# Static places and overflow tiles in a routed mixture of experts: 288 places with eight overflow tiles in place of 416 with two

## The chip, the cores and the metric

The kernel runs on one core of a Trainium2 chip. The metric is device time in microseconds for one execution, the median of several; lower is better. TensorE (PE in the profile) multiplies matrices; VectorE (DVE), ScalarE (ACT) and GpSimd (POOL) do element-wise work; SyncE (SP) issues the weight loads, GpSimd the gathers and scatters of rows.

## The reference

Attention over clusters produces 3072 token rows of 512 numbers; then a mixture of eight experts takes each row to the one expert with the largest gate logit. Only the second part, cut to what matters:

```python
N, D, E, F = (3072, 512, 8, 1024)
logits = x @ w_gate
expert_idx = np.argmax(logits, axis=1)
probs = softmax(logits);  gate_w = probs[np.arange(N), expert_idx]
perm = np.argsort(expert_idx, kind='stable');  x_sorted = x[perm]
for e in range(E):
    lo, hi = (boundaries[e], boundaries[e + 1])     # rows of expert e
    h = np.maximum(x_sorted[lo:hi] @ w1[e], 0.0)    # w1[e]: 512 x 1024
    y_sorted[lo:hi] = h @ w2[e]                     # w2[e]: 1024 x 512
out = gate_w[:, None] * y_sorted[inv_perm]
```

How many rows an expert gets depends on the data. For the inputs of this case the counts are 400, 354, 531, 257, 408, 444, 274 and 404.

## The kernel before

The kernel has to be laid out before the counts are known. Each expert has a fixed number of places, full tiles of 128 and one of 32 (`RQ`). Rows that find no place go to overflow tiles of 128, each of one expert, whose number is read from a register at run time. `XU` such tiles are unrolled; a loop behind them takes any others. A place without a token is computed all the same, and its result is not stored.

```python
XU = 2
RQ = 32
FT = (2, 1)          # tiles of experts 0 and 1 that are done early, from the first three batches
NJ = N // E // P     # 3 full tiles
CAP = NJ * P + RQ    # 416 places
NC = E * (NJ + 1) + NX
```

Token numbers of all places come from one-hot matrices: VectorE and GpSimd make them, TensorE multiplies them (`tokens`), VectorE turns the product into indices. `NC` columns for tiles; the GpSimd product is 6 * NC elements a time.

The first layer of a group is either plain (`layer1`) or, by seven half-size products instead of eight, `layer1_s`. The second layer is `pair_s` (seven products over two full tiles), `layer2` for a full tile alone, and `quarters` for the 32 places, in four column groups:

```python
def layer1(g, fbs):
    cols = sum(g["n"])
    per = min(512 // cols, (fbs[1] - fbs[0]) // 2)
    for f0 in range(fbs[0], fbs[1], 2 * per):
        hp = wide()                                  # PSUM tile of two banks, three buffers
        ...                                          # 4 matmuls a block of 128 features
        for a in range(2):
            if a == 0 and not g.get("scalar_only"):
                nc.vector.tensor_relu(dst, src)
            else:
                nc.scalar.activation(dst, src, AF.Relu)

def quarters(g):
    ...                                              # matmuls into zq, four strips of 32 rows
    for t in range(1, P // RQ):
        nc.scalar.copy(zc[:, t, :], zq[t * RQ : (t + 1) * RQ, :])
    nc.vector.tensor_tensor(zc[:, 0, :], zc[:, 1, :], zq[0:RQ, :], op=ALU.add)
    for t in range(2, P // RQ):
        nc.vector.tensor_tensor(zc[:, 0, :], zc[:, 0, :], zc[:, t, :], op=ALU.add)
    rows_out(g, last, RQ, zc[:, 0, :])               # ScalarE scales by the gate, GpSimd scatters

def seven(mul, a, s, b, t, u, u3, view, c, ready, steps):
    nc.scalar.copy(u, product(s[1], t[1]));  more()  # more(): one step of other VectorE work
    p = product(a[0], b[0]);  add(u, u, p)
    nc.scalar.copy(c11, p);  more()
    add(u3, u, product(s[2], t[2]));  more()
    ...                                              # four products more
```

The sums that the seven products need are made on VectorE: `sums_w1` and `sums_x` (4 operations each) for the first layer, `sums_h` and `sums_w2` for the second.

Weights of one layer are a block of 2 MB; two buffers each for w1 and w2, all loads from SyncE's queue in the order of the code.

Experts 0 and 1 are started early, in the shadow of the attention of the last batch: two tiles and one tile. The main loop runs over groups: the rest of 0, the rest of 1, experts 2 to 7, and two overflow tiles.

```python
for i, g in enumerate(groups):
    if i + 1 < ng:
        n = groups[i + 1]
        steps = sums_h(g) + sums_w2(g) if by_s(i) else []
        ...                       # first layer of i + 1, with these steps between its products
    if i + 3 < ng:
        groups[i + 3]["w"] = [fetch1(groups[i + 3]["e"], i + 3)]
    n = groups[i + 2] if i + 2 < ng else None
    steps = sums_w1(n) if by_s(i + 2) else []
    ...                           # pair_s(g, steps)
    if n is not None:
        turn_of(n)                # transposes of i + 2
        if i + 4 < ng:
            gather_of(groups[i + 4])
        if by_s(i + 2):
            steps += sums_x(n)
    for f in steps:
        f()
    layer2(g, rest)               # third tile and the 32 places
    if n is not None:
        n["w"].append(fetch2(n["e"], i + 2))
```

Of the kernel before, what the change touches and what calls it, by code (L numbers as in the profile page):

```python
# [18 lines left out]

BIG = float(2**60)  # L20
NB = 6
XU = 2
RQ = 32
FT = (2, 1)
NP = sum(FT)


def in_general(tc, ident, ident_b, first_c, first_e, wpool, q, k, v, centroids, w_gate, w1, w2, out):
# [156 lines left out]
def kernel(  # L185
# [11 lines left out]
    nc = tc.nc  # L197
# [16 lines left out]
    XW = Dm + 4  # L214
    assert D == 64 and C == 16 and H * C == P and NQ % 2 == 0 and NQ * P == S and DB * P == Dm and FB * P == F

    NJ = N // E // P
    CAP = NJ * P + RQ
    NX = -(-(N - CAP) // P) + 1
    NC = E * (NJ + 1) + NX  # L220
# [41 lines left out]
    ps_o = late.enter_context(tc.tile_pool(name="ps_o", bufs=1, space=PSUM))  # L262
    ps_m = late.enter_context(tc.tile_pool(name="ps_m", bufs=1, space=PSUM))

    pools = dict(s=ps_s, rows=p1)


    def wide():
# [67 lines left out]
    def quarters(g):  # L336

        last = len(g["n"]) - 1
        zq = wide()[:, 0, :]
        n = FB * RQ // P  # L340
        for i in range(n):
            for t in range(P // RQ):
                nc.tensor.matmul(
                    zq[t * RQ : (t + 1) * RQ, :], lhsT=g["h"][:, t * n + i, last * P : last * P + RQ],
                    rhs=g["w"][1][:, t * n + i, :], start=(i == 0), stop=(i == n - 1),
                )

        zc = pools["wk"].tile([RQ, P // RQ, Dm], F32, name="zc", bufs=1)
        for t in range(1, P // RQ):
            nc.scalar.copy(zc[:, t, :], zq[t * RQ : (t + 1) * RQ, :])  # L350
        nc.vector.tensor_tensor(zc[:, 0, :], zc[:, 1, :], zq[0:RQ, :], op=ALU.add)  # L351
        for t in range(2, P // RQ):
            nc.vector.tensor_tensor(zc[:, 0, :], zc[:, 0, :], zc[:, t, :], op=ALU.add)
        rows_out(g, last, RQ, zc[:, 0, :])

    def layer2(g, tiles=None):
        for j in range(len(g["n"])) if tiles is None else tiles:
            if g["n"][j] < P:
                quarters(g)
                continue  # L360
            zp = wide()[:, 0, :]
            for fb in range(FB):
                nc.tensor.matmul(  # L363
                    zp, lhsT=g["h"][:, fb, j * P : (j + 1) * P], rhs=g["w"][1][:, fb, :],
                    start=(fb == 0), stop=(fb == FB - 1),
                )
            rows_out(g, j, P, zp)
# [48 lines left out]
        return sums_b(g["xs"], *b_of1(g))  # L416

    def sums_h(g):
        t = p1.tile([P, FB, 2 * P], F32, name="hs", bufs=1).rearrange("p a (b t) -> p a b t", t=P)
        g["hs"] = [t[:, 2 * i : 2 * i + 2].rearrange("p a b t -> p (a b) t") for i in range(4)]  # L420
        return sums_a(g["hs"], *a_of2(g))

    def sums_w2(g):
# [43 lines left out]
    def layer1_s(g, steps):  # L467
        half = sum(g["n"]) // 2
        per = FH // 2

        def mul(ps, a, b):
            for f in range(FH):
                o = ps[:, f // per, f % per * half : (f % per + 1) * half]
                for c in range(KH):
                    nc.tensor.matmul(  # L475
                        o, lhsT=a[:, c, f * P : (f + 1) * P], rhs=b[:, c, :],
                        start=(c == 0), stop=(c == KH - 1),
                    )

        four = lambda t: t.rearrange("p (a f) t -> p a f t", a=2)  # L480
        part = lambda f, t: four(g["h"][:, f * FH : (f + 1) * FH, t * half : (t + 1) * half])
        u = p1.tile([P, DB, 2 * P], F32, name="xu", bufs=1).rearrange("p c t -> p (c t)")
        u3 = pools["wk"].tile([P, FB, P], F32, name="u3").rearrange("p c t -> p (c t)")
        u, u3 = (four(t[:, 0 : FH * half].rearrange("p (f t) -> p f t", t=half)) for t in (u, u3))

        c = [part(f, t) for f in range(2) for t in range(2)]
        seven(
            mul, a_of1(g), g["w1s"], b_of1(g), g["xs"], u, u3,
            lambda ps: ps[:, :, 0 : per * half].rearrange("p a (f t) -> p a f t", t=half), c,
            lambda i: nc.scalar.activation(c[i], c[i], AF.Relu), steps,  # L490
        )

    def pair_s(g, steps):
# [4 lines left out]
                    ps[:, 0, 0:DH], lhsT=a[:, f, :], rhs=b[:, f, :], start=(f == 0), stop=(f == FH - 1),  # L498
                )

        uu = p1.tile([P, 2, XW], F32, name="xg1", bufs=1)
        zo = [pools["rows"].tile([P, Dm], F32, name="zo", bufs=4) for j in range(2)]

        def ready(i):
# [13 lines left out]
    def cols_of(t, c0):  # L518
        return lambda j: t[:, c0 + j : c0 + j + 1]
# [9 lines left out]
    def place_consts():  # L529
# [6 lines left out]
        for part in parts:  # L536
            nc.gpsimd.memset(part["keep"], 1.0)
            nc.gpsimd.memset(part["keep"][:, :, 0:1], 0.0)

        nc.gpsimd.memset(firsts, 0.0)  # L540
        for e, n in enumerate(FT):
            nc.gpsimd.memset(firsts[:, e : e + 1], float(n * P))
        k_["b1off"] = iota("b1off", [P, E], [[(NJ + 1) * P, E]], -1, 0)
        k_["b2off"] = iota("b2off", [P, E], [[-(NJ + 1) * P, E]], E * (NJ + 1) * P - CAP, 0)
        k_["thr"] = iota("thr", [P, NX], [[P, NX]], CAP, 0)
        k_["kx"] = iota("kx", [1, NX], [[1, NX]], 0, 0)
        k_["iota"] = iota("iota_f", [P, P], [[1, P]], 0, 0)
        k_["tiles"] = consts.tile([P, NP], F32, name="tiles1")
        for e, n in enumerate(FT):
            for j in range(n):  # L550
                i = sum(FT[:e]) + j
                nc.gpsimd.memset(k_["tiles"][:, i : i + 1], float(e * (NJ + 1) + j))

        tok_i = consts.tile([P, B, NQ], I32, name="tok_i")
        nc.gpsimd.iota(tok_i, pattern=[[S, B], [1, NQ]], base=1, channel_multiplier=NQ)
# [90 lines left out]
    def indices(pool, ps, w, gi, si):  # L646
# [10 lines left out]
        nc.vector.tensor_copy(si, tv)  # L657

    groups1 = [
        dict(  # L660
            n=[P] * n, rows=NF * P, e=e, gi=cols_of(g_idx1, sum(FT[:e])), si=cols_of(s_idx1, sum(FT[:e])), apart=True,
            scalar_only=True,
        ) for e, n in enumerate(FT)
    ]

    msched = ExitStack()
# [1 line left out]
    with ExitStack() as actx:  # L668
# [369 lines left out]

        def gather1(i):
            g = groups1[i]  # L1040
            g["xg"] = p1.tile([P, 2, XW], F32, name="xg1", bufs=1) if i == 0 else p1.tile([P, 1, XW], F32, name="xg2", bufs=1)
            gather(g)

        def turn_rows1(i):
            g = groups1[i]
            g["xT"] = p1.tile([P, DB, 2 * P], F32, name="xu", bufs=1) if i == 0 else p1.tile([P, DB, P], F32, name="xT2", bufs=1)
            g["gate"] = p1.tile([P, FT[i]], F32, name=f"gate{i}", bufs=1)
            turn_rows(g)

        def first_half(i, f0=0, f1=FB):  # L1050
            g = groups1[i]
            if f0 == 0:
                g["w"] = weights[i]
                g["h"] = p1.tile([P, FB, 2 * P], F32, name="hs", bufs=1)
            layer1(g, (f0, f1))

        n = (NG - HP) * TG
# [43 lines left out]

    mctx = ExitStack()
    pools["sums"] = mctx.enter_context(tc.tile_pool(name="sums", bufs=1))
    with tc.tile_pool(name="sm", bufs=1) as sm:
        front, back = parts
        choose(sm, back)
# [28 lines left out]
        for t0 in range(0, NT, TQ):  # L1135
            one_hots(sm, rc, slice(t0, t0 + TQ), k_["iota"], oh_r, oh_c)
        layer2(groups1[0])
        tok_ps = ps_m.tile([P, 512], F32, name="mps")[:, 0 : 2 * NC]
        tokens(tok_ps, oh_r, oh_c, NT)
        indices(sm, tok_ps, NC, g_idx, s_idx)  # L1140
# [47 lines left out]
        g["h"] = pools["wk"].tile([P, FB, CAP], F32, name="h_sb", bufs=2)  # L1188
        layer1(g, (0, FB))

    groups = []
    for e in range(E):
        j0 = FT[e] if e < len(FT) else 0
        c0 = e * (NJ + 1) + j0
        groups.append(dict(n=[P] * (NJ - j0) + [RQ], rows=N, e=e, gi=cols_of(g_idx, c0), si=cols_of(s_idx, c0), apart=True))
    for x in range(XU):
        ex = nc.sync.value_load(xe[0:1, x : x + 1], min_val=0, max_val=E - 1)
        xc = E * (NJ + 1) + x
        groups.append(dict(n=[P], rows=N, e=ex, gi=cols_of(g_idx, xc), si=cols_of(s_idx, xc), apart=True))
    for i in range(2):  # L1200
        gather_of(groups[i])
    for i in range(2):
        groups[i]["w"] = weights[i]
    ng = len(groups)
    by_s = lambda i: 0 < i < E
    for f in sums_w1(groups[1]):
        f()
    layer2(groups1[1])
    g = groups[0]
    g["xT"] = p1.tile([P, DB, 2 * P], F32, name="xu", bufs=1)  # L1210
    turn_of(g)
    gather_of(groups[2])
    g["h"] = pools["wk"].tile([P, FB, CAP], F32, name="h_sb", bufs=2)
# [3 lines left out]
    for f in sums_x(groups[1]):  # L1217
        f()
    layer1(g, (FB // 2, FB))
    groups[2]["w"] = [fetch1(groups[2]["e"], 2)]  # L1220
    for i, g in enumerate(groups):

        if i + 1 < ng:
            n = groups[i + 1]
            steps = sums_h(g) + sums_w2(g) if by_s(i) else []
            if by_s(i + 1):
                n["h"] = pools["wk"].tile([P, FB, CAP], F32, name="h_sb", bufs=2)
                layer1_s(n, steps)
            else:
                n["scalar_only"] = True  # L1230
                for f in steps:
                    f()
                layer1_of(n)
        if i + 3 < ng:
            groups[i + 3]["w"] = [fetch1(groups[i + 3]["e"], i + 3)]
        n = groups[i + 2] if i + 2 < ng else None
        steps = sums_w1(n) if by_s(i + 2) else []
        if by_s(i):
            pair_s(g, steps)
            rest = range(2, len(g["n"]))  # L1240
        else:
            rest = range(len(g["n"]))
        if n is not None:
            turn_of(n)
            if i + 4 < ng:
                gather_of(groups[i + 4])
            if by_s(i + 2):
                steps += sums_x(n)
        for f in steps:
            f()  # L1250
        layer2(g, rest)
        if n is not None:
            n["w"].append(fetch2(n["e"], i + 2))
    msched.close()

    mctx.close()
# [54 lines left out]
```

## Time and profile before

| | |
|---|---|
| time, median of 3 (lowest to highest) | 798.7 us (798.4 to 799.66) |
| span of the profiled execution | 802.5 us |
| mean granted TensorE clock | 0.990 |
| bytes read from and written to memory | 68.26 MB, 13.68 MB |
| last output products of attention end (chain, 399.54 + 4.02) | 403.56 |
| last matmuls of the kernel end (timeline, 778.11 + 13.90) | 792.0 |

In the profile a line gives the source line, the engine, the operation and its tiles as output<-inputs; "x16" counts instructions. The chain of work that ended last is followed back from the last instruction: at each step to what released it, or to the instruction before it on its engine. Where it stays on one engine with no gap, that engine's work is what sets the time there. An idle bracket in a timeline names the wait before a group and the instruction that ended it.

### The profile page before, as it was taken

What the parts mean: (1) busy time and instruction counts of PE and PEld (TensorE: products, weight loads), DVE (VectorE), ACT (ScalarE), POOL (GpSimd) and SP (SyncE); (2) the same over time, 40 slices, a digit from 0 to 9 for tenths busy, and PEclk for the clock granted to TensorE, in tenths of its full rate; (3) what the DMA queues carried; (4) which work ended last, traced back from release to release, by engine and by line L of the source; (5) the groups of instructions that cost most, each with busy time, mean ns of one, the idle gap of its engine ahead of it and who ended that gap; (6) DMA issues with size and microseconds to landing.
All of it is one profiled execution on the core that took longest, in us unless ns stands there. A gap on an engine that the chain in (4) does not pass through costs nothing.

```text
span 802.5 us, 11975 instructions
## 1 busy us (share of the span) xinstructions
PE 774.7 (97%) x4813; PEld 505.5 (63%) x4813; DVE 484.0 (60%) x783; ACT 307.1 (38%) x479; POOL 110.1 (14%) x164
## 2 busy tenths in 40 slices
PE   6999999999999999999999899999999999999994
PEld 4545454545444544444575697989797969696861
DVE  3667667767667767787536336867484847471610
ACT  4554654554655554645510123232323232232120
POOL 2200000000000000022005423030303020101010
PEclk8999999999999999999999999999999999999998
DMA  9026420382231222201010347252525233241240
GB/s 217 2 60 238 91 60 24 117 269 60 60 98 45 57 60 60 99 2 40 1 70 37 102 150 267 105 171 105 191 105 175 105 111 154 67 178 57 99 148 17
DMA packets 76191, 81.75 MB, mean 102 GB/s; under 512 B 52831, under 2 KB 56927, under 8 KB 75616
## 3 DMA queue, kind: packets, MB, share of 16 engines
q1 hardware_dynamic: 70208, 60.82, 24.8%
q0 software_dynamic: 5248, 20.04, 7.6%
q8 instruction: 40, 0.66, 0.3%
q14 instruction: 23, 0.19, 0.1%
q10 hardware_dynamic: 672, 0.05, 0.1%
HBM read 68.26 MB, written 13.68 MB: 102 GB/s over the span
## 4 chain that ended last, share of the span: by engine, by line
PE 74%; issue 12%; DVE 7%; POOL 3%; ACT 2%; POOLq 0%; ACTq 0%; DVEq 0%
PE sps L858 15%; PE sps L475 14%; PE O L878 13%; PE sps L497 8%; PE sps L363 4%; PE sps L309 4%; PE sps L861 3%; DVE T L870 3%; PE mps L899 3%; PE sps L790 2%; PE sps L290 2%; PE sps L773 2%; POOL out_dram L327 1%; PE sps L944 1%; PE mps L912 1%
## 5 line engine op out<-in xcount | busy, mean ns | idle before, releaser
L863 ACT ACTIVATE A<-sps 128x768 f32<-128x768 f32 x192 | 153.2, 812 | 53.1 <-PE sps L861 51.9
L858 PE MATMUL sps<-qk 64*128 64x384 f32 x768 | 160.4, 496 | 0.1
L870 DVE TENSOR_TENSOR T<-T,A 128x768 f32<-128x768 f32 x128 | 122.7, 958 | 14.3 <-ACT lsT L905 0.5
L878 PE MATMUL O<-A,v_in 128*64 128x384 f32 x768 | 130.9, 490 | 0.0
L858 PEld LDWEIGHTS sps<-qk 64*128 64x128 f32 x768 | 66.9, 189 | 50.1 <-issue 42.5
L878 PEld LDWEIGHTS O<-A,v_in 128*64 128x64 f32 x768 | 52.3, 137 | 62.7 <-issue 62.6
L327 POOL DMA_INDIRECT out_dram<-zo,s_idx x34 | 33.0, 970 | 255.1 <-ACT zo L509 170.6
L363 PE MATMUL sps<-w,h_sb 128*128 128x512 f32 x144 | 63.6, 596 | 0.0
L861 PE MATMUL sps<-ohT 64*128 64x384 bf16 x384 | 63.6, 325 | 0.0
L866 DVE SCALAR_TENSOR_TENSOR T<-A 128x768 f32<-128x768 f32 x32 | 30.6, 958 | 49.3 <-ACT A L863 49.3
L475 PEld LDWEIGHTS sps<-xs,w1s 128*128 128x128 f32 x336 | 56.4, 190 | 5.7 <-issue 5.7
L475 PE MATMUL sps<-xs,w1s 128*128 128x208 f32 (+1 forms) x336 | 59.4, 333 | 0.6 <-DVE xs L385 0.6
L811 POOL TENSOR_TENSOR sim<-sim,first_c 128x384 f32<-128x384 f32 x16 | 16.0, 1000 | 263.8 <-DVE sim L810 263.8
L490 ACT ACTIVATE h_sb<-h_sb 128x832 f32<-128x832 f32 (+1 forms) x28 | 24.3, 867 | 69.8 <-DVE h_sb L431 69.8
L363 PEld LDWEIGHTS sps<-w,h_sb 128*128 128x128 f32 x144 | 26.7, 190 | 30.8 <-issue 30.6
L273 POOL DMA_INDIRECT xg<-x_rows,g_idx x34 | 36.6, 1078 | 38.5 <-ACT xgT L298 17.1
L497 PE MATMUL sps<-w2s,hs 128*128 128x256 f32 x168 | 38.6, 379 | 1.8 <-DVE w2s L385 1.8
L475 PE MATMUL sps<-xgT,w 128*128 128x208 f32 (+1 forms) x224 | 40.0, 331 | 0.0
L886 ACT COPY xT<-O 128x384 f32<-128x384 f32 x32 | 15.5, 484 | 61.6 <-PE O L878 61.6
L475 PEld LDWEIGHTS sps<-xgT,w 128*128 128x128 f32 x224 | 38.0, 190 | 0.0
L351 DVE TENSOR_TENSOR zc<-zc,sps 32x512 f32<-32x512 f32 x8 | 5.4, 675 | 53.6 <-ACT zc L350 53.6
L323 ACT ACTIVATE zo<-sps,gate 128x512 f32<-128x512 f32 x12 | 8.3, 688 | 73.9 <-PE sps L363 49.7
(246 smaller groups left out, 1063.0 us busy)
## 6 DMA issues: line engine op xcount, KB each, us to landing
w<-in_moe_w_dram SPq DMA_DIRECT2D x20, 2048.0 KB, 8.5
x_rows<-x POOLq DMA_DIRECT2D x4, 1548.0 KB
q_in<-in_q_dram SPq DMA_DIRECT2D x32, 192.0 KB, 4.5
k_in<-in_k_dram SPq DMA_DIRECT2D x32, 192.0 KB, 4.8
v_in<-in_v_dram SPq DMA_DIRECT2D x16, 384.0 KB, 3.3
xg<-x_rows,g_idx POOLq DMA_INDIRECT x34
out_dram<-zo,s_idx POOLq DMA_INDIRECT x34
csb<-in_centroids_dram ACTq DMA_DIRECT2D x1, 32.0 KB, 1.9
```

The source lines that it names most:

```text
L273: nc.gpsimd.indirect_dma_start(out=g["xg"][0:m, j, :], out_offset=None, in_=x_d[0 : g["rows"], :], in_offset=bass.IndirectOffsetOnAxis(ap= ...
L309: nc.tensor.matmul(o, lhsT=g["w"][0][:, c, fb * P : (fb + 1) * P], rhs=g["xT"][:, c, :cols], start=(c == 0), stop=(c == DB - 1),)
L327: ins = nc.gpsimd.indirect_dma_start(out=out[:, :], out_offset=bass.IndirectOffsetOnAxis(ap=g["si"](j)[0:m], axis=0), in_=zo[0:m], in_offs ...
L363: nc.tensor.matmul(zp, lhsT=g["h"][:, fb, j * P : (j + 1) * P], rhs=g["w"][1][:, fb, :], start=(fb == 0), stop=(fb == FB - 1),)
L475: nc.tensor.matmul(o, lhsT=a[:, c, f * P : (f + 1) * P], rhs=b[:, c, :], start=(c == 0), stop=(c == KH - 1),)
L497: nc.tensor.matmul(ps[:, 0, 0:DH], lhsT=a[:, f, :], rhs=b[:, f, :], start=(f == 0), stop=(f == FH - 1),)
L858: nc.tensor.matmul(ps[:, a, 0:HS], lhsT=qk[g][r, 1, ks], rhs=qk[g][r, 0, qs], start=True, stop=False)
L861: nc.tensor.matmul(ps[:, a, 0:HS], lhsT=ohT[g][r, 1, ks], rhs=ohT[g][r, 0, qs], start=False, stop=True)
L863: nc.scalar.activation(A[u], ps[:, :, 0:HS], AF.Exp)
L866: nc.vector.scalar_tensor_tensor(T[g, half], in0=A[u - 1], scalar=1e-9 / P, in1=A[u], op0=ALU.add, op1=ALU.add)
L870: nc.vector.tensor_tensor(T[g, half], T[g, half], A[u], op=ALU.add)
L878: nc.tensor.matmul(O[g, half][a * D : (a + 1) * D, 0:HS], lhsT=rows[g, "v"][:, a, j, :], rhs=a_[:, a, :], start=(j == 0), stop=(j == NQ - 1),)
```

## The change

The fixed places of an expert go from 416 (three tiles and 32) to 288 (two tiles and 32), and the unrolled overflow tiles from two to eight. What a place costs is paid whether a token fills it or not; tiles whose expert is chosen at run time can be given to the experts that need them. With 288 places, the counts above need 1, 1, 2, 0, 1, 2, 0 and 1 overflow tiles.

All 288 places of expert 0 are now done early, with 128 of expert 1. Static and overflow groups alternate, so that the sums on VectorE for a static group lie beside an overflow tile, which has none, and the transposes come before the second layer, so that the sums of the next static group's rows are made between its products. Each overflow tile brings its own two blocks of weights, so 12 more are loaded.

```diff
-XU = 2
+XU = 8
 RQ = 32
-FT = (2, 1)
-NP = sum(FT)
+FT = ((128, 128, RQ), (128,))
+
+NP = sum(len(n) for n in FT)
...
-    NJ = N // E // P
+    NJ = 2
     CAP = NJ * P + RQ
...
-        zc = pools["wk"].tile([RQ, P // RQ, Dm], F32, name="zc", bufs=1)
+        zc = pools["rows"].tile([RQ, P // RQ, Dm], F32, name="zc", bufs=1)
...
+    pools["rows"] = mctx.enter_context(tc.tile_pool(name="moe_out", bufs=1))
+    w_s = [fetch1(len(FT), 0)]
...
         layer2(groups1[0])
+        w_s.append(fetch2(len(FT), 0))
         tok_ps = ps_m.tile([P, 512], F32, name="mps")[:, 0 : 2 * NC]
...
+    groups = [static(1, 1)]
+    for x, e in enumerate(range(len(FT), E)):
+        groups += [static(e, 0), overflow(x)]
+    groups += [overflow(x) for x in range(E - len(FT), XU)]
...
+    def fetch1_of(i):
+        groups[i]["e"] = groups[i]["e"]()
+        groups[i]["w"] = [fetch1(groups[i]["e"], i + 1)]
...
         if i + 1 < ng:
-            n = groups[i + 1]
-            steps = sums_h(g) + sums_w2(g) if by_s(i) else []
-            if by_s(i + 1):
-                n["h"] = pools["wk"].tile([P, FB, CAP], F32, name="h_sb", bufs=2)
-                layer1_s(n, steps)
+            n1["h"] = pools["wk"].tile([P, FB, CAP], F32, name="h_sb", bufs=2)
+            if n1["s"]:
+                layer1_s(n1, [])
             else:
-                n["scalar_only"] = True
-                for f in steps:
-                    f()
-                layer1_of(n)
+                layer1(n1, (0, FB))
         if i + 3 < ng:
-            groups[i + 3]["w"] = [fetch1(groups[i + 3]["e"], i + 3)]
...
+            fetch1_of(i + 3)
+        if i + 2 < ng:
+            turn_of(n2)
             if i + 4 < ng:
                 gather_of(groups[i + 4])
...
+        steps = sums_w1(n2) + sums_x(n2) if n2["s"] else []
+        if n1["s"]:
+            for f in sums_h(n1) + sums_w2(n1):
+                f()
+        if g["s"]:
+            pair_s(g, steps)
+            layer2(g, range(2, len(g["n"])))
+        else:
+            for f in steps:
+                f()
+            layer2(g)
+        if i + 2 < ng:
+            n2["w"].append(fetch2(n2["e"], i + 3))
```

An overflow group has `scalar_only`, so both evictions of its first layer are on ScalarE.

More of the change, by code (lines that the diff above doesn't have):

```diff
@@ L263 @@
     ps_m = late.enter_context(tc.tile_pool(name="ps_m", bufs=1, space=PSUM))
-    pools = dict(s=ps_s, rows=p1)
+    pools = dict(s=ps_s)
     def wide():
@@ L418, in sums_h @@
     def sums_h(g):
-        t = p1.tile([P, FB, 2 * P], F32, name="hs", bufs=1).rearrange("p a (b t) -> p a b t", t=P)
-        g["hs"] = [t[:, 2 * i : 2 * i + 2].rearrange("p a b t -> p (a b) t") for i in range(4)]
+        t = p1.tile([P, FB, CAP], F32, name="hs", bufs=1).rearrange("p a t -> p (a t)")
+        g["hs"] = [t[:, i * FH * P : (i + 1) * FH * P].rearrange("p (f t) -> p f t", t=P) for i in range(4)]
         return sums_a(g["hs"], *a_of2(g))
@@ L481, in layer1_s @@
         part = lambda f, t: four(g["h"][:, f * FH : (f + 1) * FH, t * half : (t + 1) * half])
-        u = p1.tile([P, DB, 2 * P], F32, name="xu", bufs=1).rearrange("p c t -> p (c t)")
+        u = p1.tile([P, DB, CAP], F32, name="xu", bufs=1).rearrange("p c t -> p (c t)")
         u3 = pools["wk"].tile([P, FB, P], F32, name="u3").rearrange("p c t -> p (c t)")
@@ L499, in mul @@
                 )
-        uu = p1.tile([P, 2, XW], F32, name="xg1", bufs=1)
+        uu = p1.tile([P, NJ + 1, XW], F32, name="xg1", bufs=1)
         zo = [pools["rows"].tile([P, Dm], F32, name="zo", bufs=4) for j in range(2)]
@@ L538, in place_consts @@
             nc.gpsimd.memset(part["keep"][:, :, 0:1], 0.0)
+        assert len(FT[0]) == NJ + 1 and len(FT) == 2
         nc.gpsimd.memset(firsts, 0.0)
         for e, n in enumerate(FT):
-            nc.gpsimd.memset(firsts[:, e : e + 1], float(n * P))
+            nc.gpsimd.memset(firsts[:, e : e + 1], float(sum(n)))
         k_["b1off"] = iota("b1off", [P, E], [[(NJ + 1) * P, E]], -1, 0)
@@ L547, in place_consts @@
         k_["iota"] = iota("iota_f", [P, P], [[1, P]], 0, 0)
[L548 to L552, printed above, removed]
+        k_["tiles"] = k_["iota"]
         tok_i = consts.tile([P, B, NQ], I32, name="tok_i")
@@ L659 @@
     groups1 = [
[L660 to L663, printed above, removed]
+        dict(n=list(n), rows=NF * P, gi=cols_of(g_idx1, c), si=cols_of(s_idx1, c), apart=True, scalar_only=True)
+        for n, c in zip(FT, (0, len(FT[0])))
     ]
@@ L1040, in gather1 @@
             g = groups1[i]
-            g["xg"] = p1.tile([P, 2, XW], F32, name="xg1", bufs=1) if i == 0 else p1.tile([P, 1, XW], F32, name="xg2", bufs=1)
+            g["xg"] = p1.tile([P, NJ + 1, XW], F32, name="xg1", bufs=1) if i == 0 else p1.tile([P, 1, XW], F32, name="xg2", bufs=1)
             gather(g)
@@ L1045, in turn_rows1 @@
             g = groups1[i]
-            g["xT"] = p1.tile([P, DB, 2 * P], F32, name="xu", bufs=1) if i == 0 else p1.tile([P, DB, P], F32, name="xT2", bufs=1)
-            g["gate"] = p1.tile([P, FT[i]], F32, name=f"gate{i}", bufs=1)
+            g["xT"] = p1.tile([P, DB, CAP], F32, name="xu", bufs=1) if i == 0 else p1.tile([P, DB, P], F32, name="xT2", bufs=1)
+            g["gate"] = p1.tile([P, len(FT[i])], F32, name=f"gate{i}", bufs=1)
             turn_rows(g)
@@ L1053, in first_half @@
                 g["w"] = weights[i]
-                g["h"] = p1.tile([P, FB, 2 * P], F32, name="hs", bufs=1)
+                g["h"] = p1.tile([P, FB, CAP], F32, name="hs", bufs=1)
             layer1(g, (f0, f1))
@@ L1189, in layer1_of, with static, overflow @@
         layer1(g, (0, FB))
-    groups = []
-    for e in range(E):
-        j0 = FT[e] if e < len(FT) else 0
+    def static(e, j0):
         c0 = e * (NJ + 1) + j0
[L1195 to L1199, printed above, removed]
+        return dict(
+            n=[P] * (NJ - j0) + [RQ], rows=N, e=lambda: e, gi=cols_of(g_idx, c0), si=cols_of(s_idx, c0), apart=True, s=j0 == 0
+        )
+    def overflow(x):
+        c0 = E * (NJ + 1) + x
+        return dict(
+            n=[P], rows=N, e=lambda: nc.sync.value_load(xe[0:1, x : x + 1], min_val=0, max_val=E - 1),
+            gi=cols_of(g_idx, c0), si=cols_of(s_idx, c0), apart=True, s=False, scalar_only=True,
+        )
+    groups = [static(1, 1)]
+    for x, e in enumerate(range(len(FT), E)):
+        groups += [static(e, 0), overflow(x)]
+    groups += [overflow(x) for x in range(E - len(FT), XU)]
+    ng = len(groups)
+    def fetch1_of(i):
+        groups[i]["e"] = groups[i]["e"]()
+        groups[i]["w"] = [fetch1(groups[i]["e"], i + 1)]
     for i in range(2):
         gather_of(groups[i])
[L1202 to L1205, printed above, removed]
+    groups[0]["w"], groups[1]["w"] = weights[1], w_s
     for f in sums_w1(groups[1]):
@@ L1209 @@
     g = groups[0]
-    g["xT"] = p1.tile([P, DB, 2 * P], F32, name="xu", bufs=1)
+    g["xT"] = p1.tile([P, DB, CAP], F32, name="xu", bufs=1)
     turn_of(g)
@@ L1219 @@
     layer1(g, (FB // 2, FB))
-    groups[2]["w"] = [fetch1(groups[2]["e"], 2)]
+    fetch1_of(2)
     for i, g in enumerate(groups):
+        n1 = groups[i + 1] if i + 1 < ng else dict(s=False)
+        n2 = groups[i + 2] if i + 2 < ng else dict(s=False)
         if i + 1 < ng:
-            n = groups[i + 1]
-            steps = sums_h(g) + sums_w2(g) if by_s(i) else []
-            if by_s(i + 1):
-                n["h"] = pools["wk"].tile([P, FB, CAP], F32, name="h_sb", bufs=2)
-                layer1_s(n, steps)
-            else:
-                n["scalar_only"] = True
-                for f in steps:
-                    f()
-                layer1_of(n)
+            n1["h"] = pools["wk"].tile([P, FB, CAP], F32, name="h_sb", bufs=2)
+            if n1["s"]:
+                layer1_s(n1, [])
+            else:
+                layer1(n1, (0, FB))
         if i + 3 < ng:
-            groups[i + 3]["w"] = [fetch1(groups[i + 3]["e"], i + 3)]
[L1236 to L1244, printed above, removed]
+            fetch1_of(i + 3)
+        if i + 2 < ng:
+            turn_of(n2)
             if i + 4 < ng:
                 gather_of(groups[i + 4])
[L1247 to L1253, printed above, removed]
+        steps = sums_w1(n2) + sums_x(n2) if n2["s"] else []
[11 more added lines that the diff above has]
+            n2["w"].append(fetch2(n2["e"], i + 3))
     msched.close()
```

## The prediction

> **What bounds the kernel now.** I read three views of the profile in this order. First the page, for the engine that carries the span:
>
> ```profile
> span 802.5 us, 11975 instructions
> PE 774.7 (97%) x4813; PEld 505.5 (63%) x4813; DVE 484.0 (60%) x783; ACT 307.1 (38%) x479; POOL 110.1 (14%) x164
> PE   6999999999999999999999899999999999999994
> DMA  9026420382231222201010347252525233241240
> PE 74%; issue 12%; DVE 7%; POOL 3%; ACT 2%; POOLq 0%; ACTq 0%; DVEq 0%
> w<-in_moe_w_dram SPq DMA_DIRECT2D x20, 2048.0 KB, 8.5
> ```
>
> TensorE (PE) is busy in every slice; in the right half, the expert stage, the DMA row stands at 1 to 5 tenths. A weight block of 2 MB lands 8.5 us after its issue. So the change is to be costed on TensorE first and the extra weight traffic checked for being hidden. Second, the chain that ended last, one expert in the middle of the expert stage:
>
> ```profile
> 468.44 13.72 PE sps L475 x112
> ...
> 612.20 1.85 PE sps L343 x16
> 614.06 19.89 PE sps L475 x112
> 633.95 12.09 PE sps L497 x56
> 646.03 1.67 PE sps L290 x16
> 647.71 7.06 PE sps L363 x16
> 654.77 1.85 PE sps L343 x16
> 656.62 19.89 PE sps L475 x112
> ```
>
> The columns are start, length, what. Every start is the end of the line before: 614.06 to 656.62 is 42.6 us per expert with TensorE never waiting. L475 is the seven-product first layer (416 places, products 208 wide), L497 the seven-product second layer of two tiles, L290 the transposes, L363 the third tile's second layer, L343 the 32 leftover places. A matmul leaves two records (56 products of L475 are x112). The line at 468.44 is the same first layer for expert 1, whose group holds 288 places: 13.72 us.
>
> Third, the timeline of TensorE where front and expert stage meet, and at the first overflow tile:
>
> ```profile
> 413.39 7.10 PE L309 MATMUL sps<-xu,w 128*128 128x256 f32 x32
> 420.69 13.98 PE L363 MATMUL sps<-w,hs 128*128 128x512 f32 x32
> 434.51 1.04 PE L642 MATMUL mps<-oh_c,oh_r 128*128 128x108 bf16 x18
> 437.03 0.45 PE L642 MATMUL mps<-oh_c,oh_r 128*128 128x108 bf16 x6 [1.48 <-POOL oh_c L632]
> 437.32 7.37 PE L309 MATMUL sps<-xT,w 128*128 128x128 f32 x64
> ...
> 740.26 7.41 PE L309 MATMUL sps<-xgT,w 128*128 128x128 f32 x64
> 749.44 1.96 PE L497 MATMUL sps<-w2s,hs 128*128 128x256 f32 x8 [1.77 <-DVE w2s L385]
> ```
>
> Brackets are idle time. Two waits matter: 1.48 us for GpSimd's one-hot products ahead of the index matmuls, and 1.77 us for VectorE's w2 sums at the first overflow tile, whose short first layer gives too little cover. A third, 0.63 us at 528.88, is for VectorE's x sums, made between expert 1's leftover places and the next first layer.
>
> **What the Trainium skill says.** "Perfetto Trace Analysis", section "Tensor Engine Instruction (MATMUL, LD_WEIGHTS)", says a matmul's reported end is estimated, not observed. This trace agrees: 16 records of L363 take 7.06 us in the chain, 441 ns apart, while their listed mean is 596 ns. I therefore use distances between starts only. "PSUM — Partial Sum Buffer", section "The four PSUM rules", limits one matmul's output to 512 fp32 columns, one bank. In the code this makes `512 // cols` one block per bank for a 288-place group, where 256 places get two; it changes how the evictions are cut, not the number of columns. "DMA: Bandwidth & Descriptors", section "Bandwidth", gives 341 GB/s for a 1 MB load. Here a 2 MB block takes 8.5 us to land, 247 GB/s with latency included, so I use 8.5. "TensorE: Matmul & The Clock Gate", section "Architectural detail", says ScalarE is a strict FIFO. The trace agrees: ScalarE's final scaling of the leftover places waits for VectorE's `zc` sums (17.4 us over 8 times, 2.2 the longest), and the next group's first copy stands behind it.
>
> **Who fills the places.** Counting the argmax of the reference on its own inputs gives 400, 354, 531, 257, 408, 444, 274 and 404 tokens for the experts. Over 416 places that is one tile for expert 2 and one for expert 5. Over 288 it is 1, 1, 2, 0, 1, 2, 0, 1 = 8 tiles: exactly the eight unrolled, so the loop for more stays empty. In the first three batches expert 0 has 313 tokens and expert 1 has 269, so their early 288 and 128 places are full.
>
> **Unit prices on TensorE.** A 288-place expert: first layer 13.72, second 12.09, leftovers 1.85, transposes 1.23 (the 1.67 of twelve full and four narrow ones, less 0.44 for four full ones, 731.00 to 731.44 in the timeline) = 28.89 us. An overflow tile: first layer 7.22 (64 records from 437.48 in the chain), second 7.06, transposes 0.44 = 14.72 us. A 416-place expert is 42.57.
>
> So one static group and one overflow tile cost 43.6 us, 1.0 more than the 416 places they stand for: the third tile loses the seven-for-eight saving in its first layer. The gain lies in places that nobody fills. All groups held 8 x 416 + 2 x 128 = 3584 places before and 8 x 288 + 8 x 128 = 3328 after.
>
> **The change part by part.** From 468.44 on, before: second layer of expert 0's remainder (7.06 + 1.85 = 8.91), expert 1 without transposes 27.66, six experts at 42.57 = 255.42, two overflow tiles 29.44: 321.4 us. The trace ends on TensorE at 778.11 + 13.90 = 792.0, thus 323.6; the 2.2 above the sum are about the waits 1.77 and 0.63. After: expert 1's remainder is now 128 + 32 places, again 8.91; expert 2 without transposes 27.66; five experts at 28.89 = 144.45; eight overflow tiles 117.76: 298.8 us. Step one is -22.6 us.
>
> Both waits of this stage should go, -2.4 us. The x sums now run inside the second-layer products before they are needed. The h and w2 sums (4 x 0.69 + 4 x 1.22 = 7.6 us of VectorE) lie beside an overflow tile's second layer and the next one's first layer, 14.3 us, with both evictions on ScalarE.
>
> The front gets longer: expert 0's first layer is 288 wide, 64 records x 32 columns x 0.85 ns = 1.7 us; its leftovers add 1.85, and four narrow transposes 0.35 (inside attention, also on TensorE). Against it, the one-hots shrink from 6 x 54 to 6 x 47 elements: eight GpSimd products of 1.03 us become some 0.9 us and the 1.48 us wait disappears, as TensorE now has 15.7 us of second layer above a chain of about 15 us. Net +2.3. ScalarE's three copies and VectorE's three additions for these leftovers stand before the index arithmetic on VectorE. That delays the indices by some 4.5 us, but the gathers have waited for `xe` anyway (7.0 us, the row POOL xg <- DVE xe), which follows expert 1's early first layer; so they slip by the same 2.3 us.
>
> New small waits: the first product of a pair needs the PSUM tile that two ScalarE evictions (1.1 us) free, with 1.23 us of transposes between; and in the next first layer the fourth product needs ScalarE's first copy done. At 526.33 in the before trace the leftovers start, and that copy ends at 534.0, 5.7 us after their end; narrower copies make it 5.5, against 3 x 1.96 = 5.9 us. I put 1.5 us for all of these over six experts.
>
> Weights: 12 more blocks. A pair takes 4 x 8.5 = 34 us of loading in 43.6 us, even one after another. The tight one is w1 of a static expert: free after the previous static first layer, needed about 0.44 + 7.06 + 7.22 + 1.23 = 16 us later by the sums. At 8.5 it is hidden with 7 us to spare. DMA share rises from 0.33 (window 614.00 to 656.60) to about 0.55.
>
> Sum: -22.6 - 2.4 + 1.5 + 2.3 + 0.4 = -20.8 us, so 798.7 - 20.8 = 777.9, rounded to 778.
>
> **Rivals.** (a) The loads become the bound. Twice the weight traffic per pair and one in-order issuing queue speak for it; the 8.5 us and the 16 us against it. If the tight w1 load took 20 us, each of six pairs would lose 4 us, 24 in all: about 802. (b) VectorE or ScalarE becomes the bound at the hand-overs. For it: the slack of 0.4 us at the fourth product, and a pair phase in which VectorE has about 9.6 of 12.1 us filled. Against it: its total falls, since six experts instead of seven need sums. One us lost per pair gives 784, two give 790. (c) The front eats more: late indices delay the first gathers beyond TensorE's cover. Some 4 us: 782. (d) More is gained than I count if the remaining idle pieces around 453 to 462 (1.08 and 1.85 us) shrink: 775.
>
> **Range and chances.** The TensorE sum is firm, built from durations in the same trace; errors are mostly one-sided, towards new waits. I take 772 to 787. Two per cent is 782.7, so 5 us of unforeseen waits may come before the verdict changes: faster 0.77, same 0.18, slower 0.05.
>
> **What would show it.** In the changed profile: a static and an overflow group repeat every 43 to 45 us on TensorE; 13.72 for x112 of L475's successor in all static groups; no wait for w2s or w1s; TensorE's last matmul near 771; DMA tenths of 4 to 7 in the expert stage. I am wrong if idle brackets before first-layer or pair products sum to over 5 us, if a wait for a weight block shows, or if the stage before expert 2's first layer is over 4 us later.

## The result and the profile after

The changed kernel takes 777.83 us, median of 4 runs (777.02 to 778.46), beside 799.18 us for the kernel before (798.4 to 800.13): a ratio of 0.9732, with a 95% interval of 0.9715 to 0.9749. In a later series, on which both stood again, it was 777.38 against 801.41 us, ratio 0.9703 (0.9689 to 0.9718). The prediction was 778.

The page of the changed kernel, the rows that answer to those of before:

```profile
span 776.7 us, 12417 instructions
PE 755.2 (97%) x5021; PEld 485.7 (63%) x5021; DVE 449.8 (58%) x758; ACT 299.0 (38%) x481; POOL 111.0 (14%) x157
DMA  9025501455115221120103446747556675847540
PE 80%; issue 9%; DVE 6%; POOL 2%; ACT 2%; ACTq 0%; POOLq 0%; DVEq 0%
w<-in_moe_w_dram SPq DMA_DIRECT2D x32, 2048.0 KB, 9.2
```

TensorE still holds the span. Its busy time fell by 19.5 us, while the weight blocks went from 20 to 32 and the DMA row of the expert stage from 1 to 5 tenths to mostly 4 to 8. A block lands in 9.2 us (median) in place of 8.5.

The chain that ended last, one static group and one overflow tile in the middle of the expert stage (start, length, what):

```profile
513.10 13.92 PE sps L476 x112
527.02 0.44 PE sps L291 x4
527.46 6.87 PE sps L364 x16
534.33 7.14 PE sps L310 x64
541.47 1.23 PE sps L291 x12
...
542.71 12.35 PE sps L498 x56
555.06 1.85 PE sps L344 x16
556.91 13.92 PE sps L476 x112
```

Seven-product first layer of a static group, then transposes, second layer and first layer of overflow tiles, then transposes, second layer and leftovers of static groups. From 513.10 to 556.91 it is 43.81 us with no waiting between the pieces. The timeline of TensorE at the front, at the first pair after an overflow tile, and at the end:

```profile
404.51 4.05 PE L310 MATMUL sps<-xu,w 128*128 128x288 f32 x16
...
414.88 8.01 PE L310 MATMUL sps<-xu,w 128*128 128x288 f32 x32
...
423.09 13.98 PE L364 MATMUL sps<-w,hs 128*128 128x512 f32 x32
437.00 1.92 PE L344 MATMUL sps<-w,hs 128*32 128x512 f32 x16
438.86 1.22 PE L641 MATMUL mps<-oh_c,oh_r 128*128 128x94 bf16 x24
439.91 7.38 PE L310 MATMUL sps<-xT,w 128*128 128x128 f32 x64
...
498.89 1.99 PE L498 MATMUL sps<-w2s,hs 128*128 128x256 f32 x8
...
752.72 13.90 PE L364 MATMUL sps<-w,h_sb 128*128 128x512 f32 x32
```

The bracket of 1.48 us before the index matmuls (L641) is gone, and so is the one of 1.77 us before the pair that follows the first overflow tile's first layer (498.89 has no bracket). In exchange there are the leftovers of expert 0 (437.00). TensorE ends at 752.72 + 13.90 = 766.6 in place of 792.0.

### The profile page after: what moved, and what is told of

Its sections match the earlier page's. It is cut to its first block, busy times and chain, and to the rows that moved or that the text cites. A ratio compares the mean times of both kernels' runs of the same rounds, so it can differ in the third digit from the quotient of the medians.

```text
span 776.7 us, 12417 instructions
## 1 busy us (share of the span) xinstructions
PE 755.2 (97%) x5021; PEld 485.7 (63%) x5021; DVE 449.8 (58%) x758; ACT 299.0 (38%) x481; POOL 111.0 (14%) x157
## 4 chain that ended last, share of the span: by engine, by line
PE 80%; issue 9%; DVE 6%; POOL 2%; ACT 2%; ACTq 0%; POOLq 0%; DVEq 0%
PE sps L855 15%; PE O L875 13%; PE sps L476 10%; PE sps L310 9%; PE sps L498 8%; PE sps L364 7%; PE sps L858 4%; PE mps L896 3%; DVE T L867 3%; PE sps L787 2%; PE sps L344 2%; PE sps L770 2%; PE sps L291 2%; PE sps L941 1%; PE mps L909 1%
## 5 line engine op out<-in xcount | busy, mean ns | idle before, releaser
L310 PEld LDWEIGHTS sps<-xgT,w 128*128 128x128 f32 x512 | 58.3, 192 | 4.5 <-issue 2.5
L310 PE MATMUL sps<-xgT,w 128*128 128x128 f32 x512 | 58.7, 275 | 0.0
L476 PEld LDWEIGHTS sps<-xs,w1s 128*128 128x128 f32 x288 | 36.0, 190 | 4.2 <-DVE xs L387 4.2
L476 PE MATMUL sps<-xs,w1s 128*128 128x144 f32 x288 | 37.8, 288 | 0.0
L858 PEld LDWEIGHTS <-ohT 64*128 64x128 bf16 x384 | 19.5, 95 | 25.3 <-issue 0.6
L297 DVE COPY xgT<-sps 128x512 f32<-128x512 f32 (+1 forms) x20 | 10.8, 566 | 40.6 <-PE sps L291 40.6
L498 PE MATMUL sps<-w2s,hs 128*128 128x256 f32 x144 | 33.6, 383 | 0.0
```

The source lines that it names most:

```text
L310: nc.tensor.matmul(o, lhsT=g["w"][0][:, c, fb * P : (fb + 1) * P], rhs=g["xT"][:, c, :cols], start=(c == 0), stop=(c == DB - 1),)
L476: nc.tensor.matmul(o, lhsT=a[:, c, f * P : (f + 1) * P], rhs=b[:, c, :], start=(c == 0), stop=(c == KH - 1),)
L498: nc.tensor.matmul(ps[:, 0, 0:DH], lhsT=a[:, f, :], rhs=b[:, f, :], start=(f == 0), stop=(f == FH - 1),)
L858: nc.tensor.matmul(ps[:, a, 0:HS], lhsT=ohT[g][r, 1, ks], rhs=ohT[g][r, 0, qs], start=False, stop=True)
```

## The experiments

The theory throughout: a place costs its TensorE time, filled or not, and the gain is the price of the 256 places saved; loads and VectorE work stay hidden. The rivals put part of the gain into the order of the groups, or have the loads take part of it back.

### The kernel before, profiled once more

The spans of the two profiles differ by 25.8 us, the medians by only 21.35. The timeline of the first profile of the kernel before shows where a part of that is, between expert 0's remainder and expert 1's first layer:

```profile
454.45 4.61 PE L309 MATMUL sps<-xu,w 128*128 128x160 f32 x32 [1.08 <-issue]
458.90 1.40 PE L290 MATMUL sps<-ident,xg 128*128 128x128 f32 x12
462.15 6.29 PE L309 MATMUL sps<-xu,w 128*128 128x160 f32 x32 [1.85 <-ACT h_sb L319]
468.27 2.12 PE L475 MATMUL sps<-xs,w1s 128*128 128x144 f32 x16
```

and its table of stretches (start and end; length, busy PE, PEld, DVE, ACT, POOL, each with counts; granted clock, DMA share, GB/s):

```profile
458.00:462.00 4.00, 2.30 (x20) 2.02 (x19) 0.86 (x2) 0.34 (x2) 1.24 (x2) 1.00 0.51 145
462.00:466.00 4.00, 3.85 (x16) 3.85 (x17) 2.07 (x6) 0.84 (x4) 2.86 (x3) 0.59 0.33 78
```

TensorE stood for 1.7 of 4 us, and in the next 4 us its granted clock was 0.59.

> The kernel before once more, for a second profile. In the first one TensorE lost about 3.7 us between 454.45 and 468.44 (a wait at expert 1's transposes and a granted clock of 0.59 after it), which the changed kernel does not lose, and the predicted 2.7 us of extra front work came out as -1.0. Theory A: that loss belongs to that one execution; here the stage from expert 0's remainder's first layer to expert 1's first layer takes about 10.4 us, and the span is 3 to 4 us below 802.5. Theory B: it belongs to the kernel; the stage takes 13 to 14 us again and the change removed a real wait.

Measured: span 797.5 us, 799.31 us for the run. The front's start, the same place and the end in the second profile, TensorE's timeline:

```profile
402.49 3.62 PE L309 MATMUL sps<-xu,w 128*128 128x256 f32 x16
...
453.07 4.61 PE L309 MATMUL sps<-xu,w 128*128 128x160 f32 x32 [1.08 <-ACT xu L298]
457.52 1.40 PE L290 MATMUL sps<-ident,xg 128*128 128x128 f32 x12
458.85 4.61 PE L309 MATMUL sps<-xu,w 128*128 128x160 f32 x32
463.30 2.12 PE L475 MATMUL sps<-xs,w1s 128*128 128x144 f32 x16
...
773.13 13.90 PE L363 MATMUL sps<-w,h_sb 128*128 128x512 f32 x32
```

453.07 to 463.30 is 10.2 us against 13.8 before (454.45 to 468.27), with no bracket at the second half. Theory A holds: not every execution has the loss. Of the 5.0 us between the two spans, 3.6 lie here and 1.4 ahead of expert 0's first early matmul (403.88 and 402.49). The second profile is the one to compare with below. What the transposes stood for in the first is not shown; a late gather of expert 1's rows would fit and was not tried.

It need not be a single accident, though. The run of the first profile took 804.3 us at a mean granted clock of 0.990. In the two later series, five of eighteen runs of the kernel before took 803.5 to 804.5 us at 0.988 to 0.992, the other thirteen 800.3 to 801.6 at 0.993 to 0.997. None of the nine runs of the changed kernel stands apart so (777.0 to 778.5). Whether those five lost their time at the same place, and whether the change removed the cause, is not shown.

### The same tiles in another order

```diff
-        groups += [static(e, 0), overflow(x)]
-    groups += [overflow(x) for x in range(E - len(FT), XU)]
+        groups += [static(e, 0)]
+    groups += [overflow(x) for x in range(XU)]
```

with the loop body of the kernel before.

> 288 places and eight tiles, but the static groups first and the eight overflow tiles after them, with the loop order of the kernel before. TensorE's instructions are the same in number. Theory (the gain is places times unit price, order is only a precaution): within 3 us of 777.8. Rival (the alternation carries part of the gain): a static group alone has about 25.6 us of VectorE work for 28.9 us of TensorE, and an overflow tile alone 4 MB of weights for 14.5 us (290 GB/s), so waits of 1 to 3 us per group appear, and the time is 788 to 810, most of the gain gone.

Measured: 780.8 us (780.09 to 781.61), ratio to before 0.977 (0.9754 to 0.9787). TensorE's timeline of this kernel, two starts of a static first layer, the change to overflow tiles, and two tiles in a row:

```profile
518.66 2.20 PE L476 MATMUL sps<-xs,w1s 128*128 128x144 f32 x16 [0.32 <-DVE xs L386]
...
548.46 2.20 PE L476 MATMUL sps<-xs,w1s 128*128 128x144 f32 x16 [0.32 <-DVE xs L386]
...
645.87 1.97 PE L498 MATMUL sps<-w2s,hs 128*128 128x256 f32 x8 [1.77 <-DVE w2s L386]
...
682.55 7.03 PE L364 MATMUL sps<-w,h_sb 128*128 128x512 f32 x16
689.42 7.31 PE L310 MATMUL sps<-xgT,w 128*128 128x128 f32 x64
...
697.00 7.03 PE L364 MATMUL sps<-w,h_sb 128*128 128x512 f32 x16
```

A static group takes 29.80 us (518.66 to 548.46), 0.9 over the 28.89 us that the prediction had priced, 0.32 of it the wait for the x sums; the old 1.77 us wait for the w2 sums is back. Overflow tiles in a row keep 14.45 us (682.55 to 697.00): 4 MB each, and no wait for a load. Beside 799.43 us for the kernel before in this series, the places without the alternation give 18.6 us, and the alternation, with the loop order that goes with it, about 3 more. The rival's 788 to 810 did not come; nor did waits of 1 to 3 us per group.

### Overflow tiles on borrowed weights

```diff
+        if not groups[i]["s"]:
+            groups[i]["w"] = [groups[i - 1]["w"][0]]
+            return
         groups[i]["e"] = groups[i]["e"]()
-        groups[i]["w"] = [fetch1(groups[i]["e"], i + 1)]
+        groups[i]["w"] = [fetch1(groups[i]["e"], groups[i]["e"])]
...
-            n2["w"].append(fetch2(n2["e"], i + 3))
+            n2["w"].append(fetch2(n2["e"], n2["e"]) if n2["s"] else n1["w"][1])
```

The 16 blocks of the overflow tiles are left out; their rows go through another expert's weights.

> The overflow tiles use the weights of the static group before them in place of their own, so their 16 blocks (33.6 MB) are not loaded; the overflow rows' results are thus of the wrong expert. Theory (all loads are hidden): within 1 us of 777.8. Rival (the doubled weight traffic takes back part of the gain): 3 to 8 us faster, 770 to 775.

Measured: 778.19 us (777.34 to 778.49), against 777.83 with all loads. The page of this run:

```profile
span 776.7 us, 12315 instructions
DMA  9025501455114221120103444614326170400000
```

The DMA row of the expert stage falls from 4 to 8 tenths to mostly 0 to 6, and the span is the same 776.7 us. The loads are hidden in full. The rival that has the loads take part of the gain back falls. A block lands in 9.4 us here with half of the loads left out, so the rise from 8.5 to 9.2 us can't be put down to the doubled traffic.

### Two tiles more, both empty

```diff
-XU = 8
+XU = 10
```

> Ten overflow tiles in place of eight, the last two without a token. Theory (a place costs its TensorE time whether filled or not: 7.14 + 6.87 + 0.44 = 14.45 us a tile in the changed kernel's steady part): +28.9 us, 806 to 808. Rival 1 (tiles in a row are bound by their two blocks, 9.2 us each): +36.8 us, 813 to 817. Rival 2 (empty tiles hide somewhere): under +20 us.

Measured: 805.97 us (805.26 to 806.61), 28.1 us more than the changed kernel. TensorE's timeline at two tiles of the row:

```profile
750.67 7.03 PE L364 MATMUL sps<-w,h_sb 128*128 128x512 f32 x16
757.54 7.31 PE L310 MATMUL sps<-xgT,w 128*128 128x128 f32 x64
764.68 0.60 PE L291 MATMUL sps<-ident,xg 128*128 128x128 f32 x4
765.12 7.03 PE L364 MATMUL sps<-w,h_sb 128*128 128x512 f32 x16
...
779.13 13.90 PE L364 MATMUL sps<-w,h_sb 128*128 128x512 f32 x32
```

14.45 us a tile. The line at 757.54 is the first layer of the first empty tile, the one at 779.13 the second layers of both empty tiles: 7.14 and 13.90 us, against 7.15 and 13.90 us for tiles with tokens in the changed kernel. So an empty place costs as much as a full one, and a tile at the end of the row is not bound by its 4 MB. Two tiles would make 28.9 us; the medians, each amid runs that spread over some 1.4 us, give 28.1.

### Transposes after the second layer again

```diff
-            turn_of(n2)
...
-        steps = sums_w1(n2) + sums_x(n2) if n2["s"] else []
+        if not g["s"]:
+            turn_n2()
+        steps = sums_w1(n2) if n2["s"] else []
...
             pair_s(g, steps)
+            turn_n2()
+            if n2["s"]:
+                for f in sums_x(n2):
+                    f()
```

> The changed kernel with one thing of its order undone: the transposes and the x sums of the next static group come after the seven second-layer products again, beside the 32 leftover places only. Theory (the order saves the wait for the x sums, 0.3 to 0.6 us per static group, seen as 0.32 us in the run with the static groups first): +1.5 to +3 us, 779 to 781. Rival (the order is worth nothing, the pause only moves): within 0.7 us of 777.8.

Measured: 778.01 us (777.85 to 778.22): a miss, the rival holds. The wait is there, in its timeline:

```profile
512.06 2.20 PE L476 MATMUL sps<-xs,w1s 128*128 128x144 f32 x16 [0.32 <-DVE xs L386]
...
555.96 2.20 PE L476 MATMUL sps<-xs,w1s 128*128 128x144 f32 x16 [0.31 <-DVE xs L386]
```

but the period is 43.90 us (512.06 to 555.96), 0.1 more than with the new order. There the seven second-layer products take 12.35 us, here, in the chain,

```profile
540.47 12.09 PE sps L498 x56
```

What the new order saves before the first layer it mostly pays around the second. This part of the change is worth nothing that can be measured.

### Eviction on both engines

```diff
-            gi=cols_of(g_idx, c0), si=cols_of(s_idx, c0), apart=True, s=False, scalar_only=True,
+            gi=cols_of(g_idx, c0), si=cols_of(s_idx, c0), apart=True, s=False,
```

> The first layer of an overflow tile evicted half by VectorE and half by ScalarE in place of ScalarE alone. Theory (the first product of the pair waits for the PSUM tile of that layer, 12.35 in place of 12.09 us a pair): the wait shrinks, up to 0.26 x 6 = 1.6 us faster, 776.2 to 777.5. Rival (VectorE is then late with the h and w2 sums, or the 0.26 us are not from this wait): no change or slower, 777.5 to 780.

Measured: 778.21 us (777.62 to 778.65): no gain, the rival holds. In its timeline a wait has appeared where none was:

```profile
541.31 1.99 PE L498 MATMUL sps<-w2s,hs 128*128 128x256 f32 x8 [0.24 <-ACT h_sb L320]
```

The two halves of the eviction in the same run, VectorE's and ScalarE's:

```profile
539.87 0.69 DVE L318 TENSOR_SCALAR h_sb<-sps 128x512 f32<-128x512 f32 x1 [5.65 <-PE sps L310]
540.66 0.60 ACT L320 ACTIVATE h_sb<-sps 128x512 f32<-128x512 f32 x1 [7.24 <-DVE h_sb L318]
```

ScalarE's half starts only when VectorE's has ended, so the two take 1.39 us where ScalarE alone needs 1.08 for both, and TensorE waits 0.24 us for it. With ScalarE alone there is no bracket at this place: its evictions end at 542.65 (541.57 + 1.08) in the changed kernel and the pair starts at 542.71. So the hand-over that the prediction named is real and just covered, and the 0.26 us by which a pair is longer than in the kernel before is not a wait for this PSUM tile: behind the wait the pair still takes 12.35 us here.

### 280 places

```diff
-RQ = 32
+RQ = 24
+ST = 32
```

`ST` keeps the four column strips of the leftovers at 32.

> 280 places in place of 288 (24 in the last, partial tile; still eight overflow tiles for these counts). Theory (the time follows the columns on TensorE, 0.85 ns each per record): 112 records x 4 columns x 0.85 = 0.38 us for each of six first layers, 64 x 8 x 0.85 = 0.44 us for expert 0's and for expert 1's remainder, together 3.2 us: 774.6. Rival (records this narrow are bound by loading weights, not by columns): under 1 us, 777 to 778.

> 280 places and both engines evicting the overflow tiles' first layer. If both gains are real and lie on the path, they add: 773 to 774.5. If the hand-over at the leftovers (fourth product waiting for ScalarE's first copy, slack 0.4 us at 288) now bites with narrower products, about 1 to 2 us are lost again: 775 to 776.5.

Measured: 774.03 us (772.92 to 775.13) for 280 places, and 775.39 us (775.11 to 775.74) with both engines evicting, 1.4 us more. The timeline of the second has five waits of 0.25 us before pairs, for the same eviction, which is 1.25 of it, and no other wait that the 280 places alone lack; a loss at the leftovers' hand-over was not shown. To set 280 and 288 places on one chip, both ran once more:

> The changed kernel once more, so that it stands on the same chip as the 280-place variant. Theory: 777 to 779, and beside the 280-place variant of this call 3 to 4 us slower. The front, from expert 0's first early matmul to expert 2's first layer, takes 62.8 us again, against 60.8 us in the second profile of the kernel before: the leftovers, the wider first layer and the vanished wait together cost 2.0 us. Rival: front times scatter by more than 1 us from run to run, and then that price can't be read from single profiles.

> 280 places once more, beside the changed kernel on one chip. Theory (0.85 ns a column and record): 3.2 us below it. Rival (its first reading of 774.03 owed something to the chip): under 2 us below it.

Measured: 777.38 us (777.25 to 778.28) and 774.06 us (772.88 to 775.08), 3.3 us apart. The chain of the 280-place kernel has

```profile
639.70 13.54 PE sps L477 x112
```

13.54 in place of 13.92 us: 0.38 us for 4 columns in 112 records, as expected. With a ratio to before of 0.9664 (0.9649 to 0.9678), this is the fastest of all versions here. It is cut to these counts: over 280 places the experts have 120, 74, 251, 0, 128, 164, 0 and 124 tokens left, again eight tiles, and expert 4 fills its tile exactly.

The front came out as expected too. From expert 0's first early matmul to the first seven-product first layer (expert 2's in the changed kernel, expert 1's in the kernel before) it is 62.77 us in the changed kernel's second profile (403.42 to 466.19) and in its first (404.51 to 467.28), against 60.81 us for the kernel before (402.49 to 463.30 in its second profile).

## Why the prediction was right

The prediction said -20.8 us. Against the second profile of the kernel before, whose front has no stray wait:

| step | predicted | measured | from |
|---|---|---|---|
| expert stage, work and waits | -22.6 - 2.4 + 1.5 = -23.5 | -24.4 | 463.30 to 787.0 (773.13 + 13.90) before, 467.28 to 766.6 after |
| front | +2.3 | +2.0 | 60.81 and 62.77 |
| end, after TensorE's last matmul | 0 | -0.4 | 10.5 and 10.1 |
| sum | -20.8 with +0.4 in attention | -22.8 | |

The medians of the two series give -21.4 and -24.0. The parts that the prediction lists for the front, 1.7 + 1.85 - 1.48, add up to 2.1 and not to its 2.3. Its sign "TensorE's last matmul near 771" missed: the end is 766.6. It was 792.0 less 20.8, and those 792.0 held the 3.6 us that the first profile had lost at 458 to 466; they are 3.6 of the 4.6 us. The 0.4 us in attention can't be read: the front begins at 402.49 and 403.88 in the two profiles of before, and at 404.51 and 403.42 in two of after.

**Unit prices.** The static group's and the overflow tile's prices summed to 43.6 us a pair; it is 43.81. An overflow tile in a row takes 14.45 and not 14.72: its first layer 7.14 in place of 7.22, its second 6.87 in place of 7.06.

**The two waits.** Both are gone. The one of 0.63 us in the first profile of the kernel before:

```profile
528.88 3.05 PE L475 MATMUL sps<-xs,w1s 128*128 128x208 f32 x16 [0.63 <-DVE xs L385]
```

The same place in the changed kernel, a first layer behind leftovers, with no bracket:

```profile
513.03 2.23 PE L476 MATMUL sps<-xs,w1s 128*128 128x144 f32 x16
```

The run with static groups first brings back the 1.77 and, per group, half of the 0.63. Their removal is the part of the gain that is order, not places.

**New small waits.** I allowed 1.5 us for two hand-overs. Neither shows as a wait. The first product of the pair has no bracket, and the fourth product of the first layer starts in time, so the slack of 0.4 us was enough. What came in their place has another cause. By starts in the timelines, where no wait precedes, the same matmuls take longer when work 32 rows or columns wide (the four narrow transposes, the leftovers) stands directly before or after them. For the second layer of a full tile it is 6.87 us with none beside it (527.46 in the chain of the changed kernel), and in the kernel before 7.06 with both and 6.96 with leftovers alone:

```profile
647.64 7.13 PE L363 MATMUL sps<-w,h_sb 128*128 128x512 f32 x16
654.70 1.92 PE L343 MATMUL sps<-w,h_sb 128*32 128x512 f32 x16
...
731.44 7.03 PE L363 MATMUL sps<-w,h_sb 128*128 128x512 f32 x16
738.40 1.92 PE L343 MATMUL sps<-w,h_sb 128*32 128x512 f32 x16
```

A pair takes 12.09 with none beside it (before), 12.19 with leftovers behind it (716.98 to 729.17 after), 12.28 with both (542.71 to 554.99 after; the chain says 12.35). A 288-place first layer takes 13.72 behind full-width work and 13.83 behind leftovers (513.03 to 526.86; the chain says 13.92). So in these pieces each such border costs about 0.1 us; why, is not shown. The prediction read 13.72 and 12.09 where there was no border and 7.06 where there were two, and the new order moved the borders. By the same starts, from 467.28 to 766.62, the eight overflow tiles cost 116.0 us in place of 117.8 and the rest 183.4 in place of 181.0. Two errors of about 2 us cancel, and 0.5 us is left where I had allowed 1.5: that this part of the sum came out so close is luck.

**Loads.** Hidden, as argued: the landing time of 9.2 us is still within the 16. The DMA share is 0.62 to 0.65 in the stretches of one pair each; I had put 0.55.

**The front.** The bracket of 1.48 us went, and the gathers slipped along with TensorE, as said: the first one starts 44.6 us after the front's first matmul, against 42.6 before. Of the two waits that rival (d) hoped to shrink, the 1.08 us is unchanged (457.05 in the changed kernel's timeline); the 1.85 us was missing from the second profile of the kernel before, and should not have been counted among what a change may win.

## What to carry to other kernels

Where TensorE carries a stage without gaps, price the change in TensorE time per tile from starts, empty places included, each piece read between the neighbours that it will have after the change; then look for what would break the cover, and test it by leaving that traffic out. Fixed places plus run-time tiles should be sized so that the counts just fit: here each column in the static groups was worth 0.4 us over all of them (3.3 us for 8), while the order of the groups, together with the loop order, was worth 3 us and the place of the transposes alone nothing. Eight tiles fit the counts here exactly, with 288 places as with 280; what an input that needs a ninth costs was not measured. Profile the old kernel twice before reading a difference of a few microseconds from one stage.

## What was not expected

In the first profile of the kernel before, TensorE waited 1.85 us at 462.15, and the 32 matmuls behind the wait took 6.29 us in place of 4.61, with a granted clock of 0.59 from 462 to 466. Wait and slow matmuls together lost 3.6 us. That such a pause always brings the low clock is not so: from 748 to 752 of the same profile TensorE is busy for 2.56 of 4 us (2.30 at 458 to 462), and the next 4 us have a clock of 1.00.

Splitting an eviction over two engines made it end later, not sooner (0.24 us of new wait), because the second half ran after the first. Why it waited for the first is not shown.
